# Cutting the last weight-gradient tile of a dense-SiLU backward kernel into 384 and 128 columns

## Chip, cores, metric

The kernel runs on one core of one Trainium2 chip. The metric is device time in microseconds (us) of one execution. The span of a profile is about 1.8 us shorter than that time (for the kernel before: span 321.6 us, time 323.47 us), so differences are compared within one of the two, never across them.

## The reference

Forward and backward of `silu(x @ w1) @ w2`; all data is bfloat16, and there are four outputs.

```python
B, S, D, F = 1, 2048, 640, 1536
h   = silu(einsum("bsd,df->bsf", x, w1))
out = einsum("bsf,fd->bsd", h, w2)
# outputs: out, and the gradients of x, w1, w2 for a given grad_out
```

The gradient of `w1` (`gw1`, 640 x 1536) is computed last. It is cut into 15 tiles of 128 x 512, each a sum over 16 matmuls.

## The kernel before

Only the end of the program and two pools matter for the argument. PSUM is the memory into which the matmuls here write their sums; its tiles called `hp` rotate through four banks. The output staging tiles `g1` rotate through three buffers.

```python
ps_h = tile_pool(name="ps_h", bufs=4, space=PSUM)        # each tile [128, 512] fp32 = one bank
...
            if c == 2:                                   # middle of the program: part of x
                for j in range(STC, ST, STC):            # three loads
                    nc.sync.dma_start(out=x_nat[:, j:j + STC, :], in_=x_v[:, j:j + STC, :])
...
        s1pool = fctx.enter_context(tc.tile_pool(name="s1pool", bufs=3))
...
        for fc in range(NFC):                            # 3
            gh_blk = gh_blks[fc]
            for dt_ in range(DT):                        # 5
                gp = ps_h.tile([P, FC], FP32, name="hp")
                for st in range(ST):                     # 16 matmuls, 512 columns each
                    nc.tensor.matmul(gp[:], lhsT=x_nat[:, st, dt_ * P:(dt_ + 1) * P],
                                     rhs=gh_blk[:, st, :], start=(st == 0), stop=(st == ST - 1))
                g1 = s1pool.tile([P, FC], dt_in, name="g1")
                if k % 2 == 0:
                    nc.scalar.activation(g1[:], gp[:], ACT.Copy)      # L291
                else:
                    nc.vector.tensor_copy(out=g1[:], in_=gp[:])       # L293
                k += 1
                nc.sync.dma_start(out=gw1_v[:, dt_, fc * FC:(fc + 1) * FC], in_=g1[:])   # L295
```

Of the kernel before, what the change touches and what calls it, by code (L numbers as in the profile page):

```python
# [8 lines left out]
ACT = mybir.ActivationFunctionType  # L9
ALU = mybir.AluOpType  # L10
FP32 = mybir.dt.float32
# [4 lines left out]
def kernel(  # L16
# [11 lines left out]
    nc = tc.nc  # L28
    P = 128
# [8 lines left out]
    ST, DT, FT = S // P, D // P, F // P  # L38
# [4 lines left out]
    FC = 512  # L43
    NFC = F // FC
# [3 lines left out]
    dt_in = x.dtype  # L48
# [4 lines left out]
    ps_h = ctx.enter_context(tc.tile_pool(name="ps_h", bufs=4, space=bass.MemoryType.PSUM))  # L53
# [6 lines left out]
    x_nat = natpool.tile([P, ST, D], dt_in, name="x_nat")  # L60
# [10 lines left out]
    def load_a_blk(ft, pool):  # L71
        a_blk = pool.tile([P, ST, P], dt_in, name="a_blk")
        nc.sync.dma_start_transpose(out=a_blk[:], in_=aT_scr[ft * P:(ft + 1) * P, :])
        a_blks.append(a_blk)

    with ExitStack() as mctx:
# [117 lines left out]
        for c in range(NCH):  # L194
# [14 lines left out]
            if c == 0:  # L209
                for ft in range(FT):  # L210
                    h_group(ft, xT, aT, ghT)
                nc.sync.dma_start(
                    out=aT_scr[:, c * SC:(c + 1) * SC].rearrange("(ft p) s -> p ft s", p=P), in_=aT[:]
                )
                sd_phase(c, aT, w2_nat, out_v, True)
                for ft in range(FT):
                    g_group(ft, goT, ghT)
                nc.sync.dma_start(
                    out=ghT_scr[:, c * SC:(c + 1) * SC].rearrange("(ft p) s -> p ft s", p=P), in_=ghT[:]
# [4 lines left out]
            for i in range(FT + LAG):  # L224
# [6 lines left out]
                out=aT_scr[:, c * SC:(c + 1) * SC].rearrange("(ft p) s -> p ft s", p=P), in_=aT[:]  # L231
            )
            nc.sync.dma_start(
                out=ghT_scr[:, c * SC:(c + 1) * SC].rearrange("(ft p) s -> p ft s", p=P), in_=ghT[:]
# [8 lines left out]
    with ExitStack() as fctx:  # L243
        fpool = fctx.enter_context(tc.tile_pool(name="fpool", bufs=1))
        gbpool = fctx.enter_context(tc.tile_pool(name="gbpool", bufs=NFC))
        s1pool = fctx.enter_context(tc.tile_pool(name="s1pool", bufs=3))

        ab2pool = fctx.enter_context(tc.tile_pool(name="ab2pool", bufs=FT - NAB))
        for ft in range(NAB, FT):
            load_a_blk(ft, ab2pool)  # L250
        gh_blks = []
        for fc in range(NFC):
            gh_blk = gbpool.tile([P, ST, FC], dt_in, name="gh_blk")
            nc.sync.dma_start_transpose(out=gh_blk[:], in_=ghT_scr[fc * FC:(fc + 1) * FC, :])
            gh_blks.append(gh_blk)

        gw2_sb = fpool.tile([P, FT, D], dt_in, name="gw2_sb")
        for ft in range(FT):
            a_blk = a_blks[ft]
            op_ = ps_o.tile([P, 2, 512], FP32, name="op")  # L260
            for hf in range(2):
                for st in range(ST):
                    nc.tensor.matmul(  # L263
                        op_[:, hf, 0:DH],
                        lhsT=a_blk[:, st, :],
                        rhs=go_nat[:, st, hf * DH:(hf + 1) * DH],
                        start=(st == 0),
                        stop=(st == ST - 1),
                    )
            nc.scalar.activation(  # L270
                gw2_sb[:, ft, :].rearrange("p (h d) -> p h d", h=2), op_[:, :, 0:DH], ACT.Copy
            )
        nc.sync.dma_start(out=gw2.rearrange("(ft p) d -> p ft d", p=P), in_=gw2_sb[:])

        gw1_v = gw1.rearrange("(dt p) f -> p dt f", p=P)
        k = 0
        for fc in range(NFC):
            gh_blk = gh_blks[fc]
            for dt_ in range(DT):
                gp = ps_h.tile([P, FC], FP32, name="hp")  # L280
                for st in range(ST):
                    nc.tensor.matmul(  # L282
                        gp[:],
                        lhsT=x_nat[:, st, dt_ * P:(dt_ + 1) * P],
                        rhs=gh_blk[:, st, :],
                        start=(st == 0),
                        stop=(st == ST - 1),
# [8 lines that stand above are left out]
# [30 lines left out]
```

## Time and profile before

| | |
|---|---|
| time, median of 3 | 323.47 us (323.32 to 323.51) |
| TensorE (PE) busy | 316.0 of 321.6 us, 98% |
| chain that ended last | PE 97% |
| last matmul's modelled end to end of span | 3.20 us |

From the page of before: the span, the busy table (us, share of the span, x instructions) and the chain that ended last, by engine.

```profile
span 321.6 us, 4349 instructions
...
PE 316.0 (98%) x1910; PEld 187.7 (58%) x1928; DVE 98.9 (31%) x171; ACT 79.0 (25%) x136; POOL 0.7 (0%) x6
...
PE 97%; DMA 1%; issue 0%; ACT 0%
```

The kernel is bound by TensorE, except at its very end. From the timeline of before; the columns are start, length, engine, line, operation, tiles, and in brackets the idle time before it and what ended that.

```profile
314.14 4.26 PE L282 MATMUL hp<-gh_blk,x_nat 128*128 128x512 bf16 x19
...
318.44 0.60 ACT L291 ACTIVATE g_2735<-hp 128x512 bf16<-128x512 f32 x1 [6.31 <-PE hp L282]
319.06 0.33 SPq L295 DMA_DIRECT2D out_dram<-g_2735  x1
```

When the last matmul is done, one copy (ScalarE, 597 ns), one issue of a store and one flight of that store follow in a row, and nothing else runs. From the list of DMA issues of before (KB each, and us from issue to landing):

```profile
out_dram<-g_2715 SPq DMA_DIRECT2D x1, 128.0 KB, 1.7
out_dram<-g_2735 SPq DMA_DIRECT2D x1, 128.0 KB, 1.7
```

The store lands 1.7 us after its issue. The last 0.84 us are waits and barriers that close the program. One more line of the timeline of before, from its start, is needed for the cost of short matmuls:

```profile
5.07 1.29 PE L118 MATMUL tp<-ident,x_nat 128*128 128x128 bf16 x20 [0.47 <-DMA x_nat<-in_x_dram]
```

These are 20 transposes, each a weight load and 128 columns, in 1.29 us.

### The profile page before, as it was taken

How to read it: one execution, taken by the hardware profiler on the slowest of the kernel's cores; microseconds unless marked ns; L12 is line 12 of the kernel's file. 1: busy time of each engine (PE TensorE's matmuls, PEld its weight loads, DVE VectorE, ACT ScalarE, POOL GpSimd, SP SyncE). 2: the span in 40 equal slices, each digit the busy share in tenths (PEclk: the TensorE clock that was granted, in tenths of full speed). 3: DMA queues.
4: the chain of work that ended last, by engine and by line, in shares of the span. 5: the costliest groups of instructions: out<-in, count | busy, mean ns of one | idle time of the engine just before them, and what ended most of it. 6: DMA issues, size and time to landing. Idle time of an engine off the chain costs nothing.

```text
span 321.6 us, 4349 instructions
## 1 busy us (share of the span) xinstructions
PE 316.0 (98%) x1910; PEld 187.7 (58%) x1928; DVE 98.9 (31%) x171; ACT 79.0 (25%) x136; POOL 0.7 (0%) x6
## 2 busy tenths in 40 slices
PE   8999999999999999999999999999999999999996
PEld 6467457544577644477754467777777774444442
DVE  1860553577501287800357740220000000100000
ACT  3961000445210154411054421001110111000100
POOL 0000000000000000000000000000000000000000
PEclk9999999999999999999999999999999999999999
DMA  7999999997794020292020089919999996210110
GB/s 233 318 190 198 222 278 242 369 282 269 216 293 129 12 72 0 84 309 74 9 82 0 0 264 243 230 23 237 213 188 233 266 227 231 71 49 33 35 50 33
DMA packets 113587, 52.32 MB, mean 163 GB/s; under 512 B 84000, under 2 KB 113568, under 8 KB 113568
## 3 DMA queue, kind: packets, MB, share of 16 engines
q1 hardware_dynamic: 113568, 52.04, 64.0%
q8 instruction: 15, 0.25, 0.3%
q14 instruction: 4, 0.03, 0.0%
HBM read 9.18 MB, written 21.76 MB: 96 GB/s over the span
## 4 chain that ended last, share of the span: by engine, by line
PE 97%; DMA 1%; issue 0%; ACT 0%
PE op L180 32%; PE op L263 16%; PE hp L163 16%; PE hp L282 16%; PE hp L144 16%; DMA x_nat<-in_x_dram 1%; PE tp L118 0%; ACT g_2735 L291 0%
## 5 line engine op out<-in xcount | busy, mean ns | idle before, releaser
L163 PE MATMUL hp<-goT,w2T 128*128 128x512 bf16 x238 | 56.8, 379 | 0.1
L144 PE MATMUL hp<-xT,w_nat 128*128 128x512 bf16 x229 | 56.3, 379 | 0.6
L180 PE MATMUL op<-w_nat,aT 128*128 128x320 bf16 x384 | 52.8, 299 | 0.0
L180 PE MATMUL op<-w1T,ghT 128*128 128x320 bf16 x384 | 52.8, 299 | 0.0
L263 PE MATMUL op<-go_nat,a_blk 128*128 128x320 bf16 x384 | 52.3, 299 | 0.0
L282 PE MATMUL hp<-gh_blk,x_nat 128*128 128x512 bf16 x235 | 51.7, 379 | 0.3
L151 ACT ACTIVATE aT<-hp 128x512 bf16<-128x512 f32 x48 | 28.7, 597 | 83.0 <-PE hp L144 83.0
L180 PEld LDWEIGHTS <-aT 128*128 128x128 bf16 x384 | 37.6, 98 | 15.2
L180 PEld LDWEIGHTS <-ghT 128*128 128x128 bf16 x384 | 37.6, 98 | 14.7
L263 PEld LDWEIGHTS <-a_blk 128*128 128x128 bf16 x384 | 37.6, 98 | 14.6
L163 PEld LDWEIGHTS <-w2T 128*128 128x128 bf16 x240 | 23.5, 98 | 28.1
L282 PEld LDWEIGHTS <-x_nat 128*128 128x128 bf16 x240 | 23.5, 98 | 28.2
L144 PEld LDWEIGHTS <-w_nat 128*128 128x128 bf16 x240 | 23.5, 98 | 27.7
L170 DVE SCALAR_TENSOR_TENSOR ghT<-ghT,hp 128x512 bf16<-128x512 bf16 x48 | 32.5, 682 | 16.1 <-PE hp L163 16.1
L191 DVE CAST o_sb<-op 128x640 bf16<-128x640 f32 x16 | 13.2, 825 | 78.6 <-PE op L180 78.6
L156 DVE SCALAR_TENSOR_TENSOR ghT<-aT,v 128x512 bf16<-128x512 bf16 x48 | 33.0, 688 | 0.6
L153 ACT ACTIVATE t<-hp 128x512 f32<-128x512 f32 x48 | 28.4, 592 | 0.0
L155 DVE TENSOR_SCALAR v<-t 128x512 bf16<-128x512 f32 x48 | 20.5, 427 | 20.5 <-ACT t L153 20.5
L189 ACT ACTIVATE o_sb<-op 128x640 bf16<-128x640 f32 x16 | 11.2, 703 | 49.1 <-PE op L180 49.1
L270 ACT ACTIVATE gw_sb<-op 128x640 bf16<-128x640 f32 x12 | 8.4, 703 | 56.8 <-PE op L263 56.8
L293 DVE CAST g_2475<-hp 128x512 bf16<-128x512 f32 x1 | 0.7, 691 | 58.2 <-PE hp L282 58.2
L90 PE MATMUL wp<-warm 128*128 128x128 bf16 x36 | 3.6, 293 | 1.0 <-DVE warm L85 1.0
(28 smaller groups left out, 19.6 us busy)
## 6 DMA issues: line engine op xcount, KB each, us to landing
aT_scr<-aT SPq DMA_DIRECT2D x4, 1536.0 KB, 6.3
ghT_scr<-ghT SPq DMA_DIRECT2D x4, 1536.0 KB, 9.6
out_dram<-o_sb SPq DMA_DIRECT2D x8, 640.0 KB, 4.0
x_nat<-in_x_dram SPq DMA_DIRECT2D x4, 640.0 KB, 5.5
go_nat<-in_grad_out_dram SPq DMA_DIRECT2D x4, 640.0 KB, 7.0
w_nat<-in_w_dram SPq DMA_DIRECT2D x2, 960.0 KB, 11.7
out_dram<-gw_sb SPq DMA_DIRECT2D x1, 1920.0 KB, 6.9
w_nat<-in_w_dram SPq DMA_DIRECT2D x2, 640.0 KB, 8.2
```

The lines of the kernel that those rows point to most:

```text
L144: nc.tensor.matmul(hp[:], lhsT=w1_nat[:, dt_, ft * P:(ft + 1) * P], rhs=xT[:, dt_, :], start=(dt_ == 0), stop=(dt_ == DT - 1),)
L151: nc.scalar.activation(aT[:, ft, :], hp[:], ACT.Silu)
L153: nc.scalar.activation(t[:], hp[:], ACT.Tanh, scale=0.5)
L155: nc.vector.tensor_scalar(out=v[:], in0=t[:], scalar1=-0.5, scalar2=0.5, op0=ALU.mult, op1=ALU.add)
L156: nc.vector.scalar_tensor_tensor(out=ghT[:, ft, :], in0=aT[:, ft, :], scalar=1.0, in1=v[:], op0=ALU.subtract, op1=ALU.mult)
L163: nc.tensor.matmul(gp[:], lhsT=w2T[:, dt_, ft * P:(ft + 1) * P], rhs=goT[:, dt_, :], start=(dt_ == 0), stop=(dt_ == DT - 1),)
L170: nc.vector.scalar_tensor_tensor(out=ghT[:, ft, :], in0=ghT[:, ft, :], scalar=1.0, in1=gp[:], op0=ALU.add, op1=ALU.mult)
L180: nc.tensor.matmul(op_[:, hf, 0:DH], lhsT=lhs_all[:, ft, sl * P:(sl + 1) * P], rhs=rhs_all[:, ft, hf * DH:(hf + 1) * DH], start=(ft == 0), ...
L189: nc.scalar.activation(dst, op_[:, :, 0:DH], ACT.Copy)
L191: nc.vector.tensor_copy(out=dst, in_=op_[:, :, 0:DH])
L263: nc.tensor.matmul(op_[:, hf, 0:DH], lhsT=a_blk[:, st, :], rhs=go_nat[:, st, hf * DH:(hf + 1) * DH], start=(st == 0), stop=(st == ST - 1),)
L282: nc.tensor.matmul(gp[:], lhsT=x_nat[:, st, dt_ * P:(dt_ + 1) * P], rhs=gh_blk[:, st, :], start=(st == 0), stop=(st == ST - 1),)
```

## The change

The intent is that three quarters of the last tile are copied and stored while TensorE still works on the last quarter, so that only a quarter is left to copy and store after the last matmul. The second group uses another PSUM bank, so the copy of the first need not keep TensorE waiting.

```diff
             for dt_ in range(DT):
+                if fc == NFC - 1 and dt_ == DT - 1:
+                    for k, (lo, hi) in enumerate(((0, FC - P), (FC - P, FC))):
+                        gp = ps_h.tile([P, FC], FP32, name="hp")
+                        for st in range(ST):
+                            nc.tensor.matmul(
+                                gp[:, lo:hi],
+                                lhsT=x_nat[:, st, dt_ * P:(dt_ + 1) * P],
+                                rhs=gh_blk[:, st, lo:hi],
+                                start=(st == 0),
+                                stop=(st == ST - 1),
+                            )
+                        g1 = s1pool.tile([P, FC], dt_in, name="g1")
+                        if k == 0:
+                            nc.scalar.activation(g1[:, lo:hi], gp[:, lo:hi], ACT.Copy)
+                        else:
+                            nc.vector.tensor_copy(out=g1[:, lo:hi], in_=gp[:, lo:hi])
+                        nc.sync.dma_start(
+                            out=gw1_v[:, dt_, fc * FC + lo:fc * FC + hi], in_=g1[:, lo:hi]
+                        )
+                    continue
                 gp = ps_h.tile([P, FC], FP32, name="hp")
```

## The prediction

> **What bounds the kernel now.** TensorE. The page's busy table gives PE 316.0 us of a 321.6 us span (98%), and the chain that ended last is 97% PE. The change touches only the end. The timeline of before reads there: the last matmul ends and the ACT copy (128x512) starts at 318.44; it takes 597 ns; the store is issued at 319.06 (333 ns on the SP queue) and lands 1.7 us after issue, about 320.8; barriers end the program at 321.6. So 3.16 us lie after the last matmul, all serial. Only this tail can shrink.
>
> **What the change removes, adds and moves.**
>
> 1. Matmuls. By windows cut at the tile copies, one tile of 512 columns takes 3.45 us, 216 ns a matmul; the 320-column matmuls take 26.08 us per 192, 136 ns. The slope, 0.416 ns a column, gives 162 ns at 384 columns: 16 x 162 = 2.60 us. The 128-column group loads the same 16 weights again (98 ns each in the records). Were loads not overlapped this would cost over 0.6 us. But the 20 transposes at the start, also load plus 128 columns, take 1.29 us to the end of the last (219 ns): (1.29-0.22)/19 = 56 ns a pair, so loads hide even there. This agrees with the Trainium skill, "TensorE: Matmul & The Clock Gate", section "Wait - 56ns, not 53.3ns?" (55.6 ns at N=128); its section "Back-to-back issue gap" has 81 ns for load-matmul pairs, which this trace does not support. I take 56. The last matmul's record is also shorter (219 against 379 ns). Last end after the tile's start: 15x216+379 = 3.62 us before, 2.60+15x56+219 = 3.66 after: +0.04 us.
> 2. The last copy. ACT 597 ns for 512 columns becomes DVE for 128. DVE takes 691 ns for 512 and 825 for 640: 1.05 ns a column, about 155 fixed, so about 290 ns: -0.31 us. The 384-column ACT copy (about 490 ns, by 597 and 703) starts about 0.9 us before the last matmul ends, so it and its 333 ns issue are over before the second copy ends; the separate bank lets it overlap the second group's matmuls.
> 3. The last store. 128 rows of 256 B instead of 1 KB. In before the data moves for about 0.5 us of the 1.7 us (windows of 0.2 us: 319.75 to 320.3). Packets of 256 B in the transposes took 18 ns each against 46 for 1 KB; 8 rows an engine save about 0.2 us. The rest, some 1.2 us, is fixed. The first store is issued some 0.7 us earlier and doesn't collide.
>
> **On the critical path:** all three: +0.04 - 0.31 - 0.2 = about -0.5 us of 323.47, 0.15%. Buffers (three g1, four hp) are free long before.
>
> **Predicted time:** 323.0 us, range 322.6 to 323.5. Faster by over 2%: 0.01; within 2%: 0.98; slower by over 2%: 0.01.
>
> **What would show each step.** Right: last group's matmuls about 56 ns apart; last DVE copy near 290 ns; last store landing 1.4 to 1.6 us after issue; last matmul to end of span 2.65 us instead of 3.16. Wrong: matmuls at 80 to 110 ns (weight loads bind); landing still 1.7 us or longer; the second store's issue waiting on the first.
>
> **What would make it wrong.** Weight loads that bind at 128 columns would cost 0.4 to 0.8 us and turn the gain into nothing or a small loss. A landing that doesn't shrink leaves -0.25 us, near the 0.2 us spread of the three runs.

## More of the kernel before

The framework assigns the semaphores, counters that one engine or DMA raises and another waits for. Every DMA takes the next of eight DMA semaphores (DMAHW0 to DMAHW7) in turn.

## The result, and the profile after

The time after is 323.08 us (median of 4, 322.96 to 323.60), before in the same rounds 323.49 us (median of 4, 323.32 to 323.99). The ratio is 0.9988, 95% interval 0.9974 to 1.0002. A ratio is the mean time of one kernel's fast runs over that of the other's of the same rounds, so it is not quite the ratio of these medians. By time alone the gain is not clear of noise; the traces have to show it.

From the page of after:

```profile
span 321.2 us, 4386 instructions
...
PE 316.2 (98%) x1926; PEld 188.5 (59%) x1944; DVE 99.1 (31%) x172; ACT 78.9 (25%) x136; POOL 0.7 (0%) x6
...
PE 97%; DMA 1%; issue 0%; DVE 0%; DVEq 0%
```

From its timeline (same columns):

```profile
314.77 3.66 PE L284 MATMUL hp<-gh_blk,x_nat 128*128 128x384 bf16 x32
...
317.57 0.49 ACT L293 ACTIVATE g_2735<-hp 128x384 bf16<-128x384 f32 x1 [5.46 <-PE hp L284]
318.09 0.33 SPq L296 DMA_DIRECT2D out_dram<-g_2735  x1
318.52 0.29 DVE L295 CAST g_2755<-hp 128x128 bf16<-128x128 f32 x1 [2.80 <-PE hp L284]
318.84 0.33 SPq L296 DMA_DIRECT2D out_dram<-g_2755  x1
```

From its list of DMA issues:

```profile
out_dram<-g_2735 SPq DMA_DIRECT2D x1, 96.0 KB, 1.6
...
out_dram<-g_2755 SPq DMA_DIRECT2D x1, 32.0 KB, 1.4
```

The ScalarE copy of 384 columns starts at 317.57 and its store is issued at 318.09, both before TensorE is done. After the last matmul there is a VectorE copy of 291 ns, and a store of 32 KB that lands in 1.4 us.

The records of the trace have a resolution of 1 ns, so I cut the end of each kernel into terms. "Tail" is the time from the first matmul of the last `gw1` tile to the end of the span. The profile estimates the end of a matmul rather than recording it; this modelled end of the last matmul is used for the first two terms, and a landing is the last of the store's 16 landing events.

| term, us | before | after | difference |
|---|---|---|---|
| first matmul to end of last matmul | 3.616 | 3.657 | +0.041 |
| to start of last copy | 0.037 | 0.091 | +0.054 |
| last copy | 0.597 | 0.291 | -0.306 |
| to issue of last store | 0.026 | 0.028 | +0.002 |
| issue to landing | 1.703 | 1.440 | -0.263 |
| landing to end of span | 0.840 | 0.945 | +0.105 |
| tail | 6.819 | 6.452 | -0.367 |

The spans differ by 0.383 us; the remaining 0.016 us lie before the tail. Two rows were not in the prediction: the last copy starts later, and the program takes longer to end once everything has landed. Together they take back 0.16 us.

For the first of them, the chain of after in order of time says what stands between the matmul and the copy (start, us, what):

```profile
314.94 3.51 PE hp L284 x32
318.44 0.04 DVEq L295
318.48 0.04 issue
318.52 0.29 DVE g_2755 L295
```

The same view of before:

```profile
313.87 4.55 PE hp L282 x21
318.42 0.02 issue
318.44 0.60 ACT g_2735 L291
```

Before has 0.02 us between them. After has a step of VectorE's sequencer (DVEq) and then 0.04 us more. The list of dependencies in the compiled program of after shows why that may be. An instruction with several waits gets separate wait instructions ahead of it, and keeps the last of its list itself:

```
VectorE  g1_2475 <- hp_2458   512 columns  waits DMAHW6, DMAHW7, DMAHW3, PE
VectorE  g1_2715 <- hp_2698   512 columns  waits DMAHW0, DMAHW3, PE, Activation
VectorE  g1_2755 <- hp_2738   128 columns  waits DMAHW2, DMAHW5, PE, Activation
ScalarE  g1_2735 <- hp_2718   384 columns  waits DMAHW1, DMAHW4, DVE, PE
```

Where PE stands last, the copy starts 36 to 39 ns after the matmul (all eight ScalarE copies of `gw1` in before, and the first VectorE one). Where another wait stands after PE, it starts 92 to 93 ns after (the other six VectorE copies of before). The alternative is that VectorE is simply slower to start than ScalarE.

For the second, the compiled program ends, on the sync engine, with these waits in this order, in before as in after:

```
(DMAHW3, DMAHW2)  (DMAHW4, DMAHW1)  (DMAHW5, DMAHW0)  (DMAHW6, DVE)  (DMAHW7, Activation)
```

In before the last store has DMAHW7 and is in the fifth. The change adds one DMA, so the last store moves on to DMAHW0, which is in the third; two waits that are long satisfied are still to be stepped through. From the view by source line of after, the last line of the program, within 320.28 to 320.53 us (columns: engine, operation, count, duration in ns min/median/max, first and last start), and then the same view of before, within 320.70 to 320.92 us:

```profile
L341 SPq EVENT_SEMAPHORE  x3: 28/28/949, 319.4 to 320.4; - x3
L341 SPq DRAIN  x1: 13/13/13, 320.5 to 320.5; - x1
```

```profile
L321 SPq DRAIN  x2: 7/10/12, 320.9 to 320.9; - x2
L321 SPq EVENT_SEMAPHORE  x1: 28/28/28, 320.8 to 320.8; - x1
```

In after, one of three waits lasted 949 ns, until the store had landed at 320.28, and two more of 28 ns follow it, with a drain after them. In before, whose store landed at 320.77, one wait of 28 ns and then the drains are left.

### The profile page after: what moved, and what is told of

Read it like the earlier page. It is cut to its first block, busy times and chain, and to the rows that moved or that the text cites. A ratio compares the mean times of both kernels' runs of the same rounds, so it can differ in the third digit from the quotient of the medians.

```text
span 321.2 us, 4386 instructions
## 1 busy us (share of the span) xinstructions
PE 316.2 (98%) x1926; PEld 188.5 (59%) x1944; DVE 99.1 (31%) x172; ACT 78.9 (25%) x136; POOL 0.7 (0%) x6
## 4 chain that ended last, share of the span: by engine, by line
PE 97%; DMA 1%; issue 0%; DVE 0%; DVEq 0%
PE op L180 32%; PE op L263 16%; PE hp L163 16%; PE hp L144 16%; PE hp L302 15%; DMA x_nat<-in_x_dram 1%; PE hp L284 1%; PE tp L118 0%; DVE g_2755 L295 0%; DVEq L295 0%
## 5 line engine op out<-in xcount | busy, mean ns | idle before, releaser
L302 PE MATMUL hp<-gh_blk,x_nat 128*128 128x512 bf16 x219 | 48.2, 379 | 0.3
L302 PEld LDWEIGHTS <-x_nat 128*128 128x128 bf16 x224 | 21.9, 98 | 26.3
```

## The experiments

All twelve kernels gave correct results. Every tail is measured as above. The record names four chips for the experiments (0, 3, 6 and 10); the trace of before was taken once. The matmul term repeats across the chips (3.656 or 3.657 us wherever two groups follow each other in two banks).

### again: the change once more

No edit; five rounds.

> The change once more, unaltered. 'Tail' means the time from the first matmul of the last gw1 tile to the end of the span: 6.82 us before, 6.45 us after. Theory: the tail of this run is 6.45 us within 0.02 us, and the ratio to before is 0.9985 to 0.9992. Rival: the 0.4 us is run-to-run noise of the whole program, then the tail repeats but the ratio is not distinguishable from 1 even with five rounds.

Measured: tail 6.459 us. Median 323.53 us (6 runs), before 323.84 us (11 runs), ratio 0.9989, interval 0.9976 to 1.0001. The tail repeats within 7 ns, but the rival's half about the ratio holds as well: five rounds do not tell it from 1. The reason is in the individual times. This kernel's runs fall in 323.04 to 323.38 and in 323.69 to 323.89, those of before in 323.35 to 323.49 and in 323.83 to 324.23. The profiled execution was one of the longer ones, and its list of waits for the first 20 us (engine and line, what it waited for, us in total, times, longest) ends differently from the same list of before, which is shown second:

```profile
PE wp L90 <- DVE warm L85: 1.0, 1, 1.0
PE hp L144 <- DMA w_nat<-in_w_dram: 0.6, 1, 0.6
```

```profile
PE wp L90 <- DVE warm L85: 1.0, 1, 1.0
PE tp L118 <- DMA x_nat<-in_x_dram: 0.5, 1, 0.5
```

In again, TensorE stood 0.6 us waiting for a load of `w1`. The 0.5 us of before is not its counterpart: it lies ahead of the transposes, which began at 5.07 us in before and at 5.14 us in again. The last tile began at 315.60 us in again, and at 314.79 in before; the wait is most of that. It is larger than the whole gain and has nothing to do with the change. The profiled execution of one_load_less below, a long one too, has 0.5 us of the same wait. Both kernels have the two groups of times; what the other longer executions waited for is not known, as they were not traced. This wait is not the only source of scatter: in the traces of cut_256 and same_bank (below) the last tile began 0.63 and 0.74 us later than in before without it. There most of the twenty transposes at the start followed each other every 107 ns instead of 56, and took 2.06 and 2.18 us instead of 1.29. Compared within the shorter and within the longer group, means differ by 0.25 and 0.20 us here, and by 0.39 us in both groups of the first rounds (the longer one has a single run of each kernel there), always in favour of the change; but the groups were drawn after the times were seen.

### act_last and own_buffer: why the last copy starts late

```diff
 # act_last
-                        if k == 0:
-                            nc.scalar.activation(g1[:, lo:hi], gp[:, lo:hi], ACT.Copy)
-                        else:
-                            nc.vector.tensor_copy(out=g1[:, lo:hi], in_=gp[:, lo:hi])
+                        nc.scalar.activation(g1[:, lo:hi], gp[:, lo:hi], ACT.Copy)
 # own_buffer
+        ownpool = fctx.enter_context(tc.tile_pool(name="ownpool", bufs=1))
-                        g1 = s1pool.tile([P, FC], dt_in, name="g1")
+                        g1 = (s1pool if k == 0 else ownpool).tile([P, FC], dt_in, name="g1")
```

> Both copies on ScalarE. In after, the VectorE copy started 91 ns after the modelled end of the last matmul, where ScalarE copies start 37 ns after. Theory (order of waits): the start is late when the wait for TensorE is not the last wait of the copy's list; in this kernel the list of the last copy ends with a wait on ScalarE itself, so it starts 80 to 100 ns after the last matmul although it is on ScalarE; copy about 278 ns; tail 6.42 to 6.46 us. Rival (engine): VectorE is slower to wake than ScalarE; then the last copy starts 37 ns after and the tail is about 6.38 us.

> The last copy stays on VectorE but writes into a buffer of its own, so its only wait is the one for TensorE. Theory (order of waits): it starts 37 to 40 ns after the last matmul instead of 91, copy 291 ns, tail 6.40 us. Rival (engine): it still starts about 91 ns after and the tail stays 6.45 us.

Measured (one look each): in act_last the copy took 277 ns and started 86 ns after the last matmul, although it was on ScalarE; tail 6.427 us. In own_buffer it stayed on VectorE and started 38 ns after; tail 6.388 us. The chains in order of time, act_last first:

```profile
315.02 3.51 PE hp L284 x32
318.53 0.03 ACTq L292
318.56 0.04 issue
318.60 0.28 ACT g L292
```

```profile
315.00 3.51 PE hp L285 x32
318.50 0.02 issue
318.53 0.29 DVE g L296
```

The sequencer's extra step follows the order of the waits and not the engine. The rival has fallen in both runs. own_buffer has no separate wait instruction left, so by itself it could also mean that their mere presence costs the time; one_store (below) settles that: its last VectorE copy has one ahead of it, but keeps the wait for PE itself, and starts 38 ns after. The Trainium skill, "Perfetto Trace Analysis", section "Identifying Dependency Chains", says that an instruction which waits on several engines may have separate semaphore instructions put before it; these runs agree and add the price when the wait that ends last is in such an instruction: 53 ns on VectorE (91 against 38) and 49 ns on ScalarE (86 against 37).

### one_load_less: why the program ends later

```diff
-                for j in range(STC, ST, STC):
-                    nc.sync.dma_start(out=x_nat[:, j:j + STC, :], in_=x_v[:, j:j + STC, :])
+                nc.sync.dma_start(out=x_nat[:, STC:2 * STC, :], in_=x_v[:, STC:2 * STC, :])
+                nc.sync.dma_start(out=x_nat[:, 2 * STC:ST, :], in_=x_v[:, 2 * STC:ST, :])
```

> Two loads of x in the middle of the program are merged into one, so that the last store takes the DMA semaphore that is waited for last at the end of the program, as in before; in after it is in the third of five waits. Theory: from landing to the end of the span 0.84 us as in before, instead of 0.95 us; tail 6.35 us; the ratio to before 0.9982 to 0.9990. Rival: the 0.1 us comes from the extra store itself (one more transfer to settle), then landing to end stays 0.95 us and the tail 6.45 us.

Measured: landing to end 0.829 us, tail 6.344 us. The same view of its last line, within 321.06 to 321.20 us (the store landed at 321.07), has one wait left, as in before:

```profile
L341 SPq EVENT_SEMAPHORE  x1: 28/28/28, 321.1 to 321.1; - x1
L341 SPq DRAIN  x1: 7/7/7, 321.2 to 321.2; - x1
```

Median 323.58 us (5 runs), ratio 0.9990, interval 0.9978 to 1.0002: its runs have the two groups too, so the time decides nothing. The trace does: an edit more than 100 us before the end gave back 0.116 us at the end, because the last store got the semaphore that is waited for last. The store itself and the number of stores are those of after. The number of all DMAs is again that of before (72 for 73), but it is not the cause: same_bank and whole_group have 73 like after and close in other times. Later runs happened to put the last store's wait in other places, and they line up:

| closing waits after the one for the last store | kernels | landing to end, us |
|---|---|---|
| 0 | before, one_load_less, one_store, best | 0.840, 0.829, 0.840, 0.841 |
| 1 | same_bank | 0.880 |
| 2 | after, again, act_last, own_buffer, reversed, cut_64, cut_256, cut_64_queues | 0.944 to 0.947 |
| 3 | whole_group | 1.003 |

### one_store, whole_group, same_bank, reversed: which part of the change earns the gain

```diff
 # one_store: one g1 tile for both copies, one store after them
-                        nc.sync.dma_start(out=gw1_v[:, dt_, fc * FC + lo:fc * FC + hi], in_=g1[:, lo:hi])
+                    nc.sync.dma_start(out=gw1_v[:, dt_, fc * FC:(fc + 1) * FC], in_=g1[:])
 # whole_group: one group of 16 matmuls with 512 columns ahead of the loop over (lo, hi), both copies on ScalarE
+                    gp = ps_h.tile([P, FC], FP32, name="hp")
+                    (16 matmuls as in before)
 # same_bank
-                        gp = ps_h.tile([P, FC], FP32, name="hp")
+                        if k == 0:
+                            gp = ps_h.tile([P, FC], FP32, name="hp")
 # reversed
-                    for k, (lo, hi) in enumerate(((0, FC - P), (FC - P, FC))):
+                    for k, (lo, hi) in enumerate(((0, P), (P, FC))):
```

> Matmuls and copies stay split (384, 128), but one store of all 512 columns follows the second copy. Theory: the copy's part of the gain stays and the store's part goes. The last copy's list of waits ends with TensorE here, so it starts 37 ns after the last matmul; it takes 291 ns; the store of 128 KB lands 1.70 us after its issue instead of 1.44; landing to end 0.84 us, since the store has the semaphore waited for last. Tail 6.53 to 6.62 us (before 6.82, after 6.45). Rival: landing time does not depend on the size at this scale and 1.44 was luck; then the tail is 6.30 to 6.36 us.

> One matmul group of 512 columns as in before; then two ScalarE copies (384, 128) one behind the other and two stores. Theory: without the matmul split nothing overlaps TensorE, so the second copy ends about 4.42 us after the tile's first matmul (before: 4.25), and the second store has to wait for the 333 ns of the first one's issue; tail 6.85 to 6.98 us, no better than before's 6.82. Rival: the small last store alone makes the gain, then 6.55 to 6.65 us.

> Both groups write one PSUM tile, that is one bank. The program's dependency list shows that the second group's first matmul now waits for the ScalarE copy of the first. Theory: TensorE stands idle for the first copy (lag, 491 ns, wake-up), about 0.6 to 0.8 us from the first group's last matmul to the second group's first; tail 7.1 to 7.3 us, worse than before. Rival: the bank does not matter because the columns do not overlap; tail 6.45 us.

> 128 columns first, then 384. Theory: what counts is the size of the last piece. The matmuls take as long as in after (first start to last end 3.65 us), the last copy is 384 columns on VectorE, about 557 ns, and 96 KB land about 1.6 us after issue; tail 6.83 to 6.93 us, no gain over before. Rival: any overlapped piece helps by what it takes off, so two thirds or so of the gain stay; tail 6.55 to 6.65 us.

Measured, one look each (us; "lag" is from the modelled end of the last matmul to the start of the last copy, "wait" is from the end of the last copy to the issue of the last store):

| | end of last matmul | lag | last copy | wait | landing | to end | tail |
|---|---|---|---|---|---|---|---|
| before | 3.616 | 0.037 | 0.597 | 0.026 | 1.703 | 0.840 | 6.819 |
| after | 3.657 | 0.091 | 0.291 | 0.028 | 1.440 | 0.945 | 6.452 |
| one_store | 3.656 | 0.038 | 0.291 | 0.062 | 1.701 | 0.840 | 6.588 |
| same_bank | 4.396 | 0.092 | 0.291 | 0.027 | 1.434 | 0.880 | 7.120 |
| reversed | 3.657 | 0.091 | 0.557 | 0.027 | 1.610 | 0.944 | 6.886 |

The record of the tile's first matmul is missing from the trace of reversed; there I counted from the preceding tile's VectorE copy, which starts 0.256 us after that first matmul in before, after and again.

whole_group came to 7.087 us. Its last copy ended 4.312 us after the first matmul, but its last store was issued only at 4.594 us, behind the first store's issue; it landed 1.490 us later, and 1.003 us closed the program. It missed its range (6.85 to 6.98) by 0.11 us upwards: I had left out the third closing wait and the slower landing of a store issued right behind another. The traces show where that landing loses time. In whole_group, in cut_64 (below) and for the first store of reversed the issue took 383 ns instead of 332, and the store's first row began 0.89 to 0.90 us after the start of the issue instead of 0.83.

What follows. The copy's share is independent of the store's: one_store keeps the short copy, loses the short flight, and lies between the two kernels (its store waits for both copying engines, hence 0.062 us). A small last store without the matmul split (whole_group) gains nothing. The size of the last piece is what counts: reversed has the same matmuls and the same two pieces and is slower than before by 0.07 us. And the other bank is needed: in same_bank the second group's first matmul waits for the copy of the first, in the timeline

```profile
315.53 2.76 PE L285 MATMUL hp<-gh_blk,x_nat 128*128 128x384 bf16 x16
...
318.33 0.49 ACT L294 ACTIVATE g<-hp 128x384 bf16<-128x384 f32 x1 [5.46 <-PE hp L285]
...
318.88 1.05 PE L285 MATMUL hp<-gh_blk,x_nat 128*128 128x128 bf16 x16 [0.58 <-ACT g L294]
...
320.02 0.29 DVE L296 CAST g<-hp 128x128 bf16<-128x128 f32 x1 [3.54 <-PE hp L285]
```

with 0.58 us of idle TensorE, which ends with the ScalarE copy. This wait is put there by the program; what the hardware would do without it no run here shows.

### cut_64, cut_256, cut_64_queues: the size of the last piece

```diff
-                    for k, (lo, hi) in enumerate(((0, FC - P), (FC - P, FC))):
+                    for k, (lo, hi) in enumerate(((0, FC - 64), (FC - 64, FC))):      # cut_64, cut_64_queues
+                    for k, (lo, hi) in enumerate(((0, FC // 2), (FC // 2, FC))):      # cut_256
 # cut_64_queues also
-                        nc.sync.dma_start(
+                        (nc.scalar if k == 0 else nc.sync).dma_start(
```

> Cut at 448 and 64 columns, all else as in after. Theory: weight loads still hide behind 64-column matmuls, which follow each other every 29 to 35 ns; the last copy takes about 224 ns and the last store (16 KB) lands 1.35 to 1.42 us after issue; tail 6.28 to 6.40 us. Rival: weight loads can't follow each other faster than the 56 ns seen so far; the 64-column matmuls come every 50 to 60 ns, TensorE ends about 0.4 us later, and the tail is 6.70 to 6.80 us, all the gain gone.

> Cut at 256 and 256 columns. Theory: the sum of terms holds: the last matmul's record 273 ns instead of 219, the VectorE copy about 423 ns instead of 291, 64 KB land about 0.08 us later than 32 KB; tail 6.65 to 6.78 us. Rival: two equal pieces overlap best and the tail is under 6.45 us.

> As the 448/64 cut, but the first store is issued from ScalarE's own queue. In the 448/64 run the second store was issued 246 ns after its copy ended, because the first store's 333 ns issue on the sync queue was still under way (landing 1.49 us after issue). Theory: that collision alone made that run miss; now the second store is issued 26 to 30 ns after its copy, lands 1.35 to 1.45 us later, tail 6.25 to 6.40 us. Rival: two stores that close together hinder each other in the transfer itself; then landing takes 1.6 us or more and the tail stays above 6.5 us.

Measured, one look each:

| | end of last matmul | lag | last copy | wait | landing | to end | tail |
|---|---|---|---|---|---|---|---|
| cut_256 | 3.656 | 0.093 | 0.425 | 0.028 | 1.524 | 0.944 | 6.670 |
| after (128) | 3.657 | 0.091 | 0.291 | 0.028 | 1.440 | 0.945 | 6.452 |
| cut_64 | 3.657 | 0.093 | 0.225 | 0.246 | 1.489 | 0.945 | 6.655 |
| cut_64_queues | 3.656 | 0.093 | 0.225 | 0.027 | 1.660 | 0.944 | 6.605 |

cut_256 is where the sum of terms puts it. cut_64 missed, and so did its rival, although the tail lies near the rival's figure: the 64-column matmuls do follow each other every 29 ns, each with its own weight load, and TensorE ends when it does in after. What costs is the sync queue. The first copy (448 columns, 544 ns) now ends so late that the two stores are issued back to back, as the timeline shows with both issues merged:

```profile
318.29 0.54 ACT L293 ACTIVATE g<-hp 128x448 bf16<-128x448 f32 x1 [5.88 <-PE hp L284]
318.81 0.23 DVE L295 CAST g<-hp 128x64 bf16<-128x64 f32 x1 [2.80 <-PE hp L284]
318.86 0.81 SPq L296 DMA_DIRECT2D out_dram<-g  x2
```

The second copy is done at 319.04 and its store is issued at 319.28, 0.246 us later. My theory for cut_64_queues, that this collision alone made the run miss, fell too. The wait did go (0.027 us), but the landing took 1.660 us, 0.17 us more than in cut_64, as the rival had foretold. In cut_64_queues the first 128 B row of the small store began 0.98 us after its issue (0.90 us in cut_64; in after the first 256 B row began 0.83 us after), while the 896 B rows of the other store were still moving; in cut_64 these had ended. Another 0.09 us was lost between the last row and the landing (0.450 us, 0.363 in cut_64). That the two stores hinder each other in flight fits this but is not shown apart: the run changed two things at once, how close the stores are and that they come from two queues. Which part of the path they share is left open too. The Trainium skill, "DMA: Bandwidth & Descriptors", section "Issuing engines are not separate DMA queues", says that a second issuing engine saves only the sequencer's time; here it saved 0.22 us of that and lost 0.17 us in flight.

### best: both losses mended

The edits of own_buffer and one_load_less together; five rounds.

> The change, with the last copy into a buffer of its own and with the merged load of x, so both small losses are mended. Theory: they add up; the last copy starts 37 ns after the last matmul, landing to end is 0.83 us, tail 6.29 us (before 6.82, after 6.45), which is the 0.5 us that the prediction summed. The ratio to before 0.998 to 0.9992; single executions scatter by 0.8 us, so the times will hardly tell it from after. Rival: the two losses overlap and the tail stays at 6.34 us or more.

Measured: lag 0.038 us, landing 1.438 us, landing to end 0.841 us, tail 6.293 us. Median 322.89 us (6 runs), before 323.82 us, ratio 0.9979, interval 0.9967 to 0.9991; the ratio is just below the range expected. One run of before in these rounds took 565.75 us at a granted clock of 0.56; it counts as slow and is in no ratio. The two losses add up: 0.526 us less tail than before, where after has 0.367. Of the 0.21% in the ratio the tail explains 0.16% (0.526 of 323.8); four of six executions of best fell into the shorter group of times and only three of ten fast ones of before, which by the look of it makes up the rest: within the shorter group the means differ by 0.60 us, within the longer by 0.47. From the timeline of best:

```profile
317.62 0.49 ACT L294 ACTIVATE g<-hp 128x384 bf16<-128x384 f32 x1 [5.46 <-PE hp L285]
...
318.52 0.29 DVE L296 CAST g<-hp 128x128 bf16<-128x128 f32 x1 [2.75 <-PE hp L285]
```

## Why the prediction was right, point by point

The prediction was 323.0 us and the median 323.08 us; three of the four runs lie in its range, the fourth (323.60) just above. How near the median came is in part luck: in again the same kernel had a median of 323.53 us, just above the range, because more of its runs fell into the longer group. What holds is the mechanism: of the 0.383 us that the span falls, 0.367 come off the serial tail.

- Matmuls: predicted +0.04, measured +0.041 us. From the first matmul to the start of the last they take 3.437 us; 16 x 162 + 15 x 56 ns had been forecast, 3.43 us. Weight loads hide behind 128 columns, and in cut_64 behind 64.
- Last copy: predicted 290 ns, measured 291. Its start, however, was taken to be as prompt as before. That is a missing term, +0.054 us, shown by act_last and own_buffer to come from the order of the waits. The buffers were "free long before", as predicted, and their waits still had a price: in own_buffer, where the last copy takes a fresh buffer, the term is gone.
- Last store: predicted "about 0.2 us" less, measured 0.263. By the four sizes in the tables, landing is 1.440, 1.524, 1.610 and 1.703 us for 32, 64, 96 and 128 KB, so some 0.09 us for each 32 KB. The mechanism was right and only the size was off: the stretch in which rows move shrank from 0.522 to 0.258 us, while issue to first row (0.83 us in both) and last row to landing (0.355 and 0.351 us) stayed. Eight rows an engine at 46 less 18 ns each come to 0.22 us, rounded to 0.2.
- The end of the program was taken as unchanged. This is the other missing term, +0.105 us, shown by one_load_less and the table of closing waits.
- "Last matmul to end of span 2.65 us instead of 3.16", both counted from the start of the copy before: counted from the copy's start it is 2.70 instead of 3.17 us; counted from the matmul's modelled end, 2.80 instead of 3.20.
- "The first store doesn't collide" holds at 128 columns, with 0.39 us to spare between the end of the first issue (318.42) and the end of the second copy (318.81). It does not hold at 64.

The terms sum to -0.47 us, given as -0.5; this was a little too large: two missing terms of +0.16 us, and -0.06 us from the store. The measured -0.367 us of tail is the prediction plus these, to within the rounding of its terms.

## What to carry to other kernels

When a kernel ends in matmul, copy, store, cut the last tile so that a small piece comes last, give it a bank of its own, and leave room for the first piece's store to be issued and in flight; too small a last piece brings the two stores together and loses more than it gains (with 64 columns 0.16 us were left of the 0.37). After such an edit, look at the lists of waits: a fresh buffer for the last copy and the right turn of the semaphores for the last store were worth 0.16 us here, nearly half as much as the change itself. Gains of this size are smaller than the scatter of whole executions, so split the tail of the trace into terms rather than trust the median.

## What the Trainium skill lacked or had wrong

- "TensorE: Matmul & The Clock Gate", section "Back-to-back issue gap": its 81 ns (N=128) and 131 ns (N=512) for pairs of weight load and matmul are not what this kernel shows: 55.8 ns at 128, 215.8 ns at 512, with a new weight load each time (its section "Wait — 56ns, not 53.3ns?" has 55.6 and 215.7, right to within 0.2 ns); at 64 columns 29 ns.
- "Perfetto Trace Analysis", section "Identifying Dependency Chains": it lacks the price of the separate wait instructions. A copy starts 36 to 39 ns after the matmul when the wait for TensorE is its own and last, 86 to 94 ns after when it is in an instruction ahead of it, on VectorE and ScalarE alike.
- No page I read has the price of the waits for DMA semaphores that close a program: each one that is still to be stepped through after the last landing costs 0.04 to 0.07 us (0.84, 0.88, 0.945, 1.00 us for none to three).
- "DMA: Bandwidth & Descriptors", section "Anatomy of one DMA", fits 2.0 us plus the bytes for DMAs issued from GpSimd, and lacks such a fit for the sync queue; for stores issued from there in these runs, issue to landing is 1.44 us at 32 KB and 1.70 us at 128 KB.
